# Attention with sigmoid weights: two of three score tiles read half by ScalarE and half by VectorE, last rows of scores written ahead of the last rows of values

## The chip, the cores and the metric

One core of a Trainium2 chip. The time is the device time of one execution in microseconds (us), as the median of several runs; the kernel before takes 871.62 us (median of 3 runs, 871.44 to 872.32). One further execution was profiled.

## What is computed

A batch of 8 with 12 heads of 448 positions and head size 64 goes through an attention whose weights are sigmoids, and the result through a layer that takes the largest of three products:

```python
scores = scale * np.matmul(q, k.transpose(0, 1, 3, 2)) - np.log(S)
attn = 1.0 / (1.0 + np.exp(-scores))
attn_out = np.matmul(attn, v)
x = attn_out.transpose(0, 2, 1, 3).reshape(B * S, H * D)
h = np.maximum(np.maximum(x @ w1, x @ w2), x @ w3)
out = h @ w_out
```

A sigmoid has no row maximum and no row sum, so each score can be turned into a weight by itself as soon as it is there.

## The kernel before

The kernel has two phases. The first is the attention, the second (lines 448 to 599) the layer of products, split into blocks that are combined with seven products each. All calls go through `pin`, which keeps the instructions of each engine in the order in which the program writes them; the framework adds the semaphores. An instruction of an engine therefore waits for everything that stands ahead of it on that engine, whatever it needs itself.

The attention runs over 24 "fours" (line 363): a batch element and four heads, that is two pairs of heads g = 0 and 1. The 448 positions of keys are three chunks of 128 and a rest of 64. For each pair and chunk, `scores` (L324) writes a tile `ps_s` of 128 keys by 2 heads by 448 queries into PSUM; each head has a bank of its own (the tile is `[P, 2, 512]` in 4-byte values). It takes three terms of two matmuls, since q and k are split into a high and a low part (`qk_split`, L316, a CAST and a TENSOR_TENSOR on VectorE). The rest of all four heads goes into one tile, `last_scores` (L335). There are three buffers of `ps_s`, taken in turn:

```python
ps_s = pool(stack, "ps_s", 3, space=PSUM)
```

A score tile becomes weights by a sigmoid on ScalarE, straight out of PSUM (`sigmoid`, L309, at L311), or is first copied to SBUF by VectorE (`raw_scores`, L379, at L382) and turned into weights there, in place, later (`raw_sigmoid`, L386). A buffer is free for the score tile three further on once its reader has finished. The weights are multiplied with the values by `weigh` (L347, chunks, at L349) and `last_weigh` (L354, rest, at L358) into two tiles `ps_av`, which `finish` (L369) copies to SBUF on VectorE (L374) and stores to DRAM on the queue of SP (L375).

The loop is staggered. Iteration n starts with the scores of the second pair of n (tiles s0, s1, s2), then come those of the first pair of n + 1 (f0, f1, f2), then all `weigh` of n, then `last_weigh` of n, then the last scores of n + 1 (L), then `finish` of n. So seven score tiles go round three buffers in each iteration: s2 takes the buffer of L, f0 that of s0, f1 that of s1, f2 that of s2. ScalarE reads L, s0, s2, f0, f1 and f2; VectorE reads s1.

Between these, VectorE also splits weights of the second phase (L156, L157, in some iterations) and decodes the weights that come as 64-bit words (L180 to L189), with two steps of the decode on ScalarE (L178, L179). The loads of values (L306), of queries and keys (L301) and of raw weights (L168) stand in the same queue of SP as the stores of `finish`. In the last iteration ScalarE and VectorE make the high and low parts of the first operands of the second phase (L263, L267), behind the sigmoids and the decode of that iteration.

Of the kernel before, what the change touches and what calls it, by code (L numbers as in the profile page):

```python
# [12 lines left out]
AF = mybir.ActivationFunctionType  # L13
# [26 lines left out]
def attention_then_maxout(  # L40
# [31 lines left out]
    nc = tc.nc  # L72
    B, NK = qk.shape[0], qk.shape[1]
    S = qk.shape[3] // 2
# [4 lines left out]
    scale = 1.0 / math.sqrt(D)  # L79
    neg_log_s = -math.log(S)  # L80
    pin = tc.keep_in_program_order

    const = ctx.enter_context(tc.tile_pool(name="const", bufs=1))
    bias_s = const.tile([P, 1], F32, name="bias_s")
# [10 lines left out]
    def pool(stack, name, bufs, **kw):  # L95
        return stack.enter_context(tc.tile_pool(name=name, bufs=bufs, **kw))
# [4 lines left out]
    m_p = pool(ctx, "m", 1)  # L101
# [169 lines left out]
    def attention(stack):  # L271
# [32 lines left out]
        def load_v(b, f):  # L304
            t = v_p.tile([P, 14, D], F32, name="v")
            pin(nc.sync.dma_start(out=t, in_=v[b, f]))  # L306
            return t

        def sigmoid(ps):  # L309
            a = a_p.tile([P, 2, S], F32, name="a")  # L310
            pin(nc.scalar.activation(  # L311
                out=a, in_=ps[:, :, :S], func=AF.Sigmoid, bias=bias_s, scale=scale
            ))
            return a
# [9 lines left out]
        def scores(terms, c):  # L324
            ps = ps_s.tile([P, 2, 512], F32, name="ps_s")
            for n, (kt, qt) in enumerate(terms):
                for e in range(2):
                    r = slice(e * D, (e + 1) * D)
                    pin(nc.tensor.matmul(
                        ps[:, e, :S], kt[r, S + c * P : S + (c + 1) * P], qt[r, :S],  # L330
                        start=n == 0, stop=n == len(terms) - 1,
                    ))
            return ps

        def last_scores(ts):  # L335

            ps = ps_s.tile([P, 2, 512], F32, name="ps_s")
            for g, t in enumerate(ts):
                for e in range(2):
                    r = slice(e * D, (e + 1) * D)  # L340
                    pin(nc.tensor.matmul(  # L341
                        ps[g * D : (g + 1) * D, e, :S], t[r, S + C * P :], t[r, :S],
                        start=True, stop=True,
                    ))
            return ps

        def weigh(ps, vt, g, c, a):  # L347
            for e in range(2):
                pin(nc.tensor.matmul(  # L349
                    ps[e * D : (e + 1) * D, :S], vt[:, (g * C + c) * 2 + e], a[:, e],  # L350
                    start=c == 0, stop=False,
                ))

        def last_weigh(pss, vt, a):  # L354
            for g, ps in enumerate(pss):
                r = slice(g * D, (g + 1) * D)
                for e in range(2):
                    pin(nc.tensor.matmul(  # L358
                        ps[e * D : (e + 1) * D, :S], vt[r, 4 * C + e], a[r, e],
                        start=False, stop=True,  # L360
                    ))

        fours = [(b, f) for b in range(B) for f in range(NK // 2)]

        def load(n):
            b, f = fours[n]
            return load_qk(b, 2 * f), load_qk(b, 2 * f + 1)

        def finish(n, pss, pool=m_p, names=("m11", "m12")):  # L369
            b, f = fours[n]  # L370
            for g, ps in enumerate(pss):
                k = 2 * f + g
                o = pool.tile([P, S], F32, name=names[g])
                pin(nc.vector.tensor_copy(out=o, in_=ps[:, :S]))  # L374
                pin(nc.sync.dma_start(  # L375
                    out=x_dram[k // HALF][:, k % HALF, b * S : (b + 1) * S], in_=o
                ))

        def raw_scores(ps):  # L379

            a = a_p.tile([P, 2, S], F32, name="a")
            pin(nc.vector.tensor_copy(out=a, in_=ps[:, :, :S]))  # L382
            return a

        def raw_sigmoid(a):
            pin(nc.scalar.activation(out=a, in_=a, func=AF.Sigmoid, bias=bias_s, scale=scale))  # L386

        def split_weights():
            for _ in range(2):
                if splits:  # L390
                    w_split(*splits.pop(0), nc.vector.tensor_copy)

        xs, count = {}, len(fours)
        ts, vt = load(0), load_v(*fours[0])
        next_ts = load(1)
        first = [sigmoid(scores([(ts[0],) * 2], c)) for c in range(C)]
        second_terms = qk_split(ts[1])
        decode()
        last = sigmoid(last_scores(ts))
        for n in range(count):  # L400
            ahead = n + 1 < count
            if ahead:
                next_vt = load_v(*fours[n + 1])
                later_ts = load(n + 2) if n + 2 < count else None
            if n == 0:
                first_terms = qk_split(next_ts[0])
            second = [None] * C
            second[0] = sigmoid(scores(second_terms, 0))
            second[1] = raw_scores(scores(second_terms, 1))
            second[2] = sigmoid(scores(second_terms, 2))  # L410
            if ahead:
                second_terms = qk_split(next_ts[1])
                next_first = [sigmoid(scores(first_terms, 0))]
            raw_sigmoid(second[1])
            split_weights()
            decode()
            if ahead:
                next_first += [sigmoid(scores(first_terms, c)) for c in range(1, C)]
            if n + 2 < count:
                first_terms = qk_split(later_ts[0])  # L420

            part = n - 9
            if 0 <= part < 4 * HALF:
                k, block = divmod(part, 4)
                row, th = ((0, 1), (0, 0), (1, 1), (1, 0))[block]
                x_block(xs, x_dram, 0, row, th, k)
                x_combine(xs, ((), ("t1",), ("t2", "t3"), ("t4",))[block], (k,))
            if n == count - 1:
                t_store(xs, 0)
                for name in FIRST:  # L430
                    x_lo(*x_hi(name, xs))
            pss = [ps_av.tile([P, 512], F32, name=f"ps_av{g}") for g in range(2)]
            for g, weights in enumerate((first, second)):
                for c in range(C):
                    weigh(pss[g], vt, g, c, weights[c])
            last_weigh(pss, vt, last)
            if ahead:
                last = sigmoid(last_scores(next_ts))
                finish(n, pss)
                vt, first, next_ts = next_vt, next_first, later_ts  # L440
        assert not splits
        return xs, lambda *to: finish(len(fours) - 1, pss, *to)

    with ExitStack() as stack:
        xs, finish = attention(stack)
# [68 lines left out]
    for n, (st, p) in enumerate(visits):  # L514
        nst, np_ = visits[n + 1] if (n, 2, 0) in his else (None, None)
        if nst in (1, 2):
            xs = x_load_all(np_)
        m = {}
        for q in range(3):
            ps, p1, u2, u3 = {}, None, None, None  # L520
# [37 lines left out]
            for k, (wname, xname, bank) in enumerate(PRODUCTS):  # L558
                here = n, q, k
                first = k < 4 or bank == 1  # L560
# [34 lines left out]
                if here == (n, 0, 4) and nst in (0, LAST):  # L595
                    xs = x_load(x_dram if nst == 0 else h_dram, np_)
# [45 lines left out]
```

## Time and profile before

| | |
|---|---|
| median of 3 runs | 871.62 us |
| profiled execution | 871.12 us, of which the span of instructions 869.3 |
| busy over the span | PE 860.6 (99%), PEld 693.9 (80%), DVE 647.2 (74%), ACT 393.4 (45%), POOL 182.3 (21%) |
| attention phase | up to about 258 us |
| granted clock of TensorE | full in all 40 slices |

PE is TensorE's matmuls, PEld its loads of weights, DVE is VectorE, ACT ScalarE, POOL GpSimd, SP the queue that issues the transfers. Times of rows in order of time are a start and a duration, in us from the start of the span. In a row of groups the last parts are: number of instructions | busy us, mean ns of one | idle time of the engine before them, with what ended it. In brackets behind a row of the timeline stands the idle time before it and what ended it. Matmuls overlap, and their ends are modelled, so that the start of a matmul and the waits of the loads of weights say more than busy time.

### The profile page before, as it was taken

The page shows a single profiled execution, that of the slowest core. Times are in us where ns is not written, and L with a number is a line of the kernel's source. Part 1 is how long each engine was busy: PE and PEld are TensorE (multiplying, and loading weights), DVE is VectorE, ACT ScalarE, POOL GpSimd, SP SyncE. Part 2 cuts the span into 40 slices and gives each one's busy share as a digit, 9 for nine tenths or more (in the row PEclk, how much of TensorE's full clock was granted, in tenths as well). Part 3 has the DMA queues.
Part 4 walks back from the last instruction along what each step waited for, and adds up shares of the span by engine and source line. Part 5 has one row for each costly group of instructions (what it writes and reads, how often), then busy time and mean ns, then how long its engine had stood idle before and what let it go on. Part 6 is the DMA issues. An engine that isn't in the chain of part 4 may idle for free. (4 is left out here: it accounts for less than half of the span.)

```text
span 869.3 us, 12929 instructions
## 1 busy us (share of the span) xinstructions
PE 860.6 (99%) x4842; PEld 693.9 (80%) x4842; DVE 647.2 (74%) x899; ACT 393.4 (45%) x499; POOL 182.3 (21%) x148
## 2 busy tenths in 40 slices
PE   8999999999999999999999999999999999999998
PEld 4555454555449999999999999999999998999997
DVE  5788778877876858689696879869687797737452
ACT  6777777776672414342253444225334352423320
POOL 0100022012102662602100020210002363760700
PEclk9999999999999999999999999999999999999999
DMA  6666667776637464414846542484563516262422
GB/s 248 211 230 233 226 238 251 250 250 236 227 127 276 177 246 156 178 52 132 305 145 234 217 170 79 138 302 151 222 231 135 169 58 210 103 213 98 164 77 85
DMA packets 74478, 161.87 MB, mean 186 GB/s; under 512 B 6960, under 2 KB 53936, under 8 KB 74416
## 3 DMA queue, kind: packets, MB, share of 16 engines
q1 hardware_dynamic: 74272, 160.94, 52.1%
q8 instruction: 38, 0.62, 0.3%
q14 instruction: 24, 0.20, 0.1%
q10 hardware_dynamic: 144, 0.11, 0.0%
HBM read 109.90 MB, written 51.12 MB: 185 GB/s over the span
## 5 line engine op out<-in xcount | busy, mean ns | idle before, releaser
L311 ACT ACTIVATE a<-ps_s,bias_s 128x896 f32<-128x896 f32 x144 | 137.4, 1006 | 75.4 <-PE ps_s L341 67.9
L458 PE MATMUL ps_y<-xlo_t,whi_s 128*128 128x448 f32 x432 | 156.8, 363 | 0.0
L458 PE MATMUL ps_y<-xhi_t,wlo_s 128*128 128x448 f32 x432 | 156.6, 363 | 0.0
L458 PE MATMUL ps_y<-xhi_t,whi_s 128*128 128x448 f32 x432 | 155.9, 361 | 0.0
L349 PE MATMUL ps_av<-a,v 128*64 128x448 f32 x576 | 113.5, 543 | 0.0
L458 PE MATMUL ps_y<-xlo_b,whi_a 128*128 128x448 f32 x288 | 104.6, 363 | 0.0
L458 PE MATMUL ps_y<-xhi_b,wlo_a 128*128 128x448 f32 x288 | 104.5, 363 | 0.0
L458 PE MATMUL ps_y<-xhi_b,whi_a 128*128 128x448 f32 x288 | 103.9, 361 | 0.0
L144 POOL TENSOR_TENSOR ws_s<-ws_a,ws_a 128x384 f32<-128x384 f32 x12 | 12.9, 1072 | 404.3 <-DMA ws_a<-w_dram 309.4
L568 ACT COPY p<-ps_y 128x448 f32<-128x448 f32 x48 | 25.5, 531 | 157.4 <-PE ps_y L458 144.8
L349 PEld LDWEIGHTS ps_av<-a,v 128*64 128x64 f32 x576 | 39.2, 137 | 63.0 <-issue 59.4
L458 PEld LDWEIGHTS ps_y<-xhi_t,wlo_s 128*128 128x128 f32 x432 | 81.1, 188 | 5.8
L458 PEld LDWEIGHTS ps_y<-xhi_t,whi_s 128*128 128x128 f32 x432 | 80.9, 187 | 5.6
L458 PEld LDWEIGHTS ps_y<-xlo_t,whi_s 128*128 128x128 f32 x432 | 81.1, 188 | 4.6
L542 DVE TENSOR_TENSOR m<-ps_y,u 128x448 f32<-128x448 f32 x71 | 43.8, 621 | 51.6 <-PE ps_y L458 47.3
L232 POOL TENSOR_TENSOR xs_t<-xs_b,xs_t 128x448 f32<-128x448 f32 x48 | 64.6, 1370 | 39.1 <-DMA xs_b<-x_dram 38.7
L571 DVE TENSOR_TENSOR u<-ps_y,p 128x448 f32<-128x448 f32 x48 | 29.9, 623 | 51.8 <-PE ps_y L458 47.9
L267 DVE TENSOR_TENSOR xlo_b<-xs_b,xhi_b 128x1344 fp32r<-128x1344 f32 x42 | 68.2, 1623 | 0.0
L267 DVE TENSOR_TENSOR xlo_t<-xs_t,xhi_t 128x1344 fp32r<-128x1344 f32 x42 | 67.6, 1610 | 0.0
L540 ACT COPY m<-ps_y 128x448 f32<-128x448 f32 x24 | 12.8, 533 | 119.1 <-PE ps_y L458 111.1
L178 ACT ACTIVATE c<-wraw 128x384 f32<-128x384 f32 x48 | 26.7, 556 | 76.4 <-DVE m L548 45.5
L263 ACT CAST xhi_t<-xs_t 128x1344 fp32r<-128x1344 f32 x42 | 55.3, 1316 | 11.9 <-PE ps_y L458 7.1
(68 smaller groups left out, 1677.2 us busy)
## 6 DMA issues: line engine op xcount, KB each, us to landing
qk<-qk SPq DMA_DIRECT2D x48, 448.0 KB, 5.3
xs_b<-x_dram SPq DMA_DIRECT2D x30, 672.0 KB, 6.5
wraw<-w SPq DMA_DIRECT2D x36, 384.0 KB, 6.6
xs_t<-t_dram SPq DMA_DIRECT2D x18, 672.0 KB, 7.8
v<-v SPq DMA_DIRECT2D x24, 448.0 KB, 3.7
h_dram<-m SPq DMA_DIRECT2D x48, 224.0 KB, 1.9
xs_b<-h_dram SPq DMA_DIRECT2D x16, 672.0 KB, 6.3
outT<-m SPq DMA_DIRECT2D x47, 224.0 KB, 2.0
```

The lines of the kernel that those rows point to most:

```text
L144: pin(nc.gpsimd.tensor_tensor(out=r[name], in0=r[in0], in1=r[in1], op=op))
L178: pin(nc.scalar.activation(out=square, in_=high.bitcast(F32), func=AF.Square))
L232: pin(nc.gpsimd.tensor_tensor(out=r[name][:, k], in0=r[in0][:, k], in1=r[in1][:, k], op=ALU.subtract))
L263: pin(nc.scalar.copy(out=hi, in_=r[name]))
L267: pin(nc.vector.tensor_tensor(out=lo, in0=x, in1=hi.bitcast(F32), op=ALU.subtract))
L311: pin(nc.scalar.activation(out=a, in_=ps[:, :, :S], func=AF.Sigmoid, bias=bias_s, scale=scale))
L349: pin(nc.tensor.matmul(ps[e * D : (e + 1) * D, :S], vt[:, (g * C + c) * 2 + e], a[:, e], start=c == 0, stop=False,))
L458: pin(nc.tensor.matmul(ps[:, :S], wt[:, k * P : (k + 1) * P], xt[:, k], start=first and n == 0, stop=n == len(terms) - 1, skip_group_check ...
L540: pin(nc.scalar.copy(out=m[name], in_=y))
L542: pin(nc.vector.tensor_tensor(out=m[name], in0=y, in1=add, op=ALU.add))
L568: pin(nc.scalar.copy(out=p1, in_=ps[0][:, :S]))
L571: pin(nc.vector.tensor_tensor(out=u2, in0=ps[1][:, :S], in1=p1, op=ALU.add))
```

## The change

Four things change, all in the attention loop.

- s0 and s2 are read by two engines: VectorE copies the second head's half to SBUF, and ScalarE turns the first head's half into weights (`shared_scores`). The half that was copied gets its sigmoid in place later; that makes two such sigmoids of half the size in place of one.
- s1 is read by ScalarE alone, as the other tiles are.
- `last_scores` of n + 1 stands ahead of `last_weigh` of n, where it stood behind it.
- `finish` of n stands no longer at the end of iteration n but in iteration n + 1, one half behind the copy of s0 and the other behind the copy of s2. Its stores move with it in SP's queue, behind the loads of values, queries and keys of that iteration.

```diff
--- before.py
+++ after.py
@@ -366,31 +366,38 @@
             b, f = fours[n]
             return load_qk(b, 2 * f), load_qk(b, 2 * f + 1)
 
-        def finish(n, pss, pool=m_p, names=("m11", "m12")):
+        def finish(n, pss, pool=m_p, names=("m11", "m12"), gs=range(2)):
+            if n < 0:
+                return
             b, f = fours[n]
-            for g, ps in enumerate(pss):
+            for g in gs:
                 k = 2 * f + g
                 o = pool.tile([P, S], F32, name=names[g])
-                pin(nc.vector.tensor_copy(out=o, in_=ps[:, :S]))
+                pin(nc.vector.tensor_copy(out=o, in_=pss[g][:, :S]))
                 pin(nc.sync.dma_start(
                     out=x_dram[k // HALF][:, k % HALF, b * S : (b + 1) * S], in_=o
                 ))
 
-        def raw_scores(ps):
+        def shared_scores(ps):
 
             a = a_p.tile([P, 2, S], F32, name="a")
-            pin(nc.vector.tensor_copy(out=a, in_=ps[:, :, :S]))
+            pin(nc.vector.tensor_copy(out=a[:, 1], in_=ps[:, 1, :S]))
+            pin(nc.scalar.activation(
+                out=a[:, 0], in_=ps[:, 0, :S], func=AF.Sigmoid, bias=bias_s, scale=scale
+            ))
             return a
 
         def raw_sigmoid(a):
-            pin(nc.scalar.activation(out=a, in_=a, func=AF.Sigmoid, bias=bias_s, scale=scale))
+            pin(nc.scalar.activation(
+                out=a[:, 1], in_=a[:, 1], func=AF.Sigmoid, bias=bias_s, scale=scale
+            ))
 
         def split_weights():
             for _ in range(2):
                 if splits:
                     w_split(*splits.pop(0), nc.vector.tensor_copy)
 
-        xs, count = {}, len(fours)
+        xs, count, pss = {}, len(fours), None
         ts, vt = load(0), load_v(*fours[0])
         next_ts = load(1)
         first = [sigmoid(scores([(ts[0],) * 2], c)) for c in range(C)]
@@ -405,13 +412,16 @@
             if n == 0:
                 first_terms = qk_split(next_ts[0])
             second = [None] * C
-            second[0] = sigmoid(scores(second_terms, 0))
-            second[1] = raw_scores(scores(second_terms, 1))
-            second[2] = sigmoid(scores(second_terms, 2))
+            second[0] = shared_scores(scores(second_terms, 0))
+            finish(n - 1, pss, gs=(0,))
+            second[1] = sigmoid(scores(second_terms, 1))
+            second[2] = shared_scores(scores(second_terms, 2))
+            finish(n - 1, pss, gs=(1,))
             if ahead:
                 second_terms = qk_split(next_ts[1])
                 next_first = [sigmoid(scores(first_terms, 0))]
-            raw_sigmoid(second[1])
+            raw_sigmoid(second[0])
+            raw_sigmoid(second[2])
             split_weights()
             decode()
             if ahead:
@@ -433,11 +443,10 @@
             for g, weights in enumerate((first, second)):
                 for c in range(C):
                     weigh(pss[g], vt, g, c, weights[c])
+            next_last = sigmoid(last_scores(next_ts)) if ahead else None
             last_weigh(pss, vt, last)
             if ahead:
-                last = sigmoid(last_scores(next_ts))
-                finish(n, pss)
-                vt, first, next_ts = next_vt, next_first, later_ts
+                vt, first, next_ts, last = next_vt, next_first, later_ts, next_last
         assert not splits
         return xs, lambda *to: finish(len(fours) - 1, pss, *to)
```

What this makes of the order of instructions, at three places of the middle of the loop. Behind a row stands in brackets for which engines' semaphores the instruction waits (PE_49 for TensorE, DVE_49 for VectorE, Activation_49 for ScalarE, DMAHW for a transfer); a wait that another wait already implies is not written.

ScalarE from L on, before: `a_1545` is L, then come s0, s2 and f0, the sigmoid in place of s1 and the two steps of the decode.

```order
L311 ACTIVATE a_1545<-ps_s_1540,bias_s_58 128x896 [waits PE_49,Activation_49]
L311 ACTIVATE a_1566<-ps_s_1559,bias_s_58 128x896 [waits PE_49,Activation_49]
L311 ACTIVATE a_1584<-ps_s_1577,bias_s_58 128x896 [waits PE_49,Activation_49]
L311 ACTIVATE a_1597<-ps_s_1590,bias_s_58 128x896 [waits PE_49]
L386 ACTIVATE a_1575<-a_1575,bias_s_58 128x896 [waits DVE_49,Activation_49]
L178 ACTIVATE c_1610<-wraw_1366 128x384 [waits DMAHW3_49]
L179 ACTIVATE wraw_1366<-wraw_1366 128x384
```

After: L, the half of s0, s1, the half of s2, f0, the two sigmoids in place, the decode.

```order
L311 ACTIVATE a_1577<-ps_s_1572,bias_s_58 128x896 [waits PE_49,Activation_49]
L385 ACTIVATE a_1596<-ps_s_1589,bias_s_58 128x448 [waits DVE_49,Activation_49]
L311 ACTIVATE a_1609<-ps_s_1602,bias_s_58 128x896 [waits PE_49]
L385 ACTIVATE a_1618<-ps_s_1611,bias_s_58 128x448 [waits DVE_49,Activation_49]
L311 ACTIVATE a_1635<-ps_s_1628,bias_s_58 128x896 [waits PE_49]
L391 ACTIVATE a_1596<-a_1596,bias_s_58 128x448
L391 ACTIVATE a_1618<-a_1618,bias_s_58 128x448
L178 ACTIVATE c_1649<-wraw_1399 128x384 [waits DMAHW3_49]
L179 ACTIVATE wraw_1399<-wraw_1399 128x384
```

The full reads of s0 and s2 became halves, and the read of s1 came in between them. The two halves wait for VectorE, not for TensorE.

VectorE from the split of the first pair on, before: CAST and TENSOR_TENSOR of the split, the two copies of `finish`, the copy of s1, the next split.

```order
L320 CAST hi_1397<-qk_1321 128x896 [waits DMAHW1_49,PE_49]
L321 TENSOR_TENSOR lo_1398<-qk_1321,hi_1397 128x896 [waits DVE_49]
L374 COPY m11_1430<-ps_av0_1405 128x448 [waits DMAHW6_49,PE_49]
L374 COPY m12_1433<-ps_av1_1406 128x448 [waits DMAHW7_49,PE_49]
L382 COPY a_1458<-ps_s_1451 128x896 [waits PE_49]
L320 CAST hi_1469<-qk_1323 128x896 [waits DMAHW2_49,PE_49]
L321 TENSOR_TENSOR lo_1470<-qk_1323,hi_1469 128x896 [waits DVE_49]
```

After:

```order
L320 CAST hi_1549<-qk_1465 128x896 [waits DMAHW6_49,PE_49]
L321 TENSOR_TENSOR lo_1550<-qk_1465,hi_1549 128x896 [waits DVE_49]
L384 COPY a_1596<-ps_s_1589 128x448 [waits PE_49]
L376 COPY m11_1599<-ps_av0_1558 128x448 [waits DMAHW0_49]
L384 COPY a_1618<-ps_s_1611 128x448 [waits PE_49]
L376 COPY m12_1621<-ps_av1_1559 128x448 [waits DMAHW1_49]
L320 CAST hi_1624<-qk_1467 128x896 [waits DMAHW7_49]
L321 TENSOR_TENSOR lo_1625<-qk_1467,hi_1624 128x896 [waits DVE_49]
```

The copies of `finish` moved behind those of s0 and s2, each of which has half the size of the one of s1.

TensorE at f0 and f1, before; the first row of each tile has the waits.

```order
L329 MATMUL ps_s<-hi 128x448 [waits DVE_49,Activation_49]
L329 MATMUL ps_s<-hi 128x448
L329 MATMUL ps_s<-lo,hi 128x448 [waits DVE_49]
L329 MATMUL ps_s<-lo,hi 128x448
L329 MATMUL ps_s<-hi,lo 128x448 x2
L329 MATMUL ps_s<-hi 128x448 [waits DVE_49]
L329 MATMUL ps_s<-hi 128x448
L329 MATMUL ps_s<-lo,hi 128x448 x2
L329 MATMUL ps_s<-hi,lo 128x448 x2
L329 MATMUL ps_s<-hi 128x448 [waits Activation_49]
```

After:

```order
L329 MATMUL ps_s<-hi 128x448 [waits Activation_49]
L329 MATMUL ps_s<-hi 128x448
L329 MATMUL ps_s<-lo,hi 128x448 x2
L329 MATMUL ps_s<-hi,lo 128x448 x2
L329 MATMUL ps_s<-hi 128x448 [waits Activation_49]
L329 MATMUL ps_s<-hi 128x448
L329 MATMUL ps_s<-lo,hi 128x448 x2
L329 MATMUL ps_s<-hi,lo 128x448 x2
L329 MATMUL ps_s<-hi 128x448 [waits Activation_49]
```

f1, whose buffer was s1's, waited for VectorE, and now waits for ScalarE; f0 waits for ScalarE in both.

## The prediction

> **What bounds the kernel now.** The change touches only the attention loop, so I read first what each engine waits for between 13 and 254 us, then one iteration of the loop in order of time, from one weigh to the next (160.74 to 171.27 us). I call the seven score tiles of an iteration s0, s1, s2 (second pair of heads), f0, f1, f2 (first pair of the next iteration) and L (last rows). Three rows of the waits (engine, line, what ended the wait: total, times, longest):
>
> ```profile
> ACT a L311 <- PE ps_s L341: 67.9, 23, 3.0
> DVE a L382 <- PE ps_s L329: 23.5, 23, 1.0
> PEld ps_s L329 <- ACT a L311: 12.7, 44, 0.5
> ```
>
> ScalarE and VectorE wait for TensorE in every iteration, so neither is full. TensorE's weight loads wait for ScalarE's reads of score tiles 44 times, about twice an iteration. These waits are all that the change could win. The stretch of one iteration confirms it:
>
> ```profile
> 160.74:171.27 10.53, 10.51 (x78) 5.30 (x77) 9.11 (x16) 7.44 (x10) 1.15 (x1) 1.00 0.72 250
> ```
>
> After the length the columns are busy PE, PEld, DVE, ACT and POOL. PE's 10.51 says little, as matmuls overlap; DVE has 1.42 us to spare, ACT 3.09. TensorE's own rows (start, duration) show its pace:
>
> ```profile
> 160.74 4.73 PE L349 MATMUL ps_av<-a,v 128*64 128x448 f32 x24
> 165.41 0.98 PE L358 MATMUL ps_av<-a,v 64*64 64x448 f32 x8
> 166.21 0.93 PE L341 MATMUL ps_s<-qk 64*64 64x448 f32 x8
> 167.07 0.47 PE L329 MATMUL ps_s<-hi 64*128 64x448 f32 x2
> ...
> 167.58 0.36 PE L329 MATMUL ps_s<-hi,lo 64*128 64x448 f32 x2
> 167.78 0.37 PE L329 MATMUL ps_s<-hi 64*128 64x448 f32 x2
> ...
> 168.19 0.37 PE L329 MATMUL ps_s<-hi,lo 64*128 64x448 f32 x2
> 168.40 0.43 PE L329 MATMUL ps_s<-hi 64*128 64x448 f32 x2
> ...
> 169.25 0.47 PE L329 MATMUL ps_s<-hi 64*128 64x448 f32 x2
> ...
> 169.96 0.37 PE L329 MATMUL ps_s<-hi 64*128 64x448 f32 x2
> ...
> 170.58 0.36 PE L329 MATMUL ps_s<-hi 64*128 64x448 f32 x2
> ...
> 171.27 0.60 PE L349 MATMUL ps_av<-a,v 128*64 128x448 f32 x2
> ```
>
> The rows with hi alone start s0 (167.07), s1 (167.78), s2 (168.40), f0 (169.25), f1 (169.96), f2 (170.58); those with hi,lo at 167.58 and 168.19 are the last pairs of s0 and s1. A tile that follows without a stall comes 0.61 to 0.62 after the one before (169.96 to 170.58). From s2 to f0 it is 0.85, and f0 itself, started afresh after a stall, takes 0.71 to f1. A loop without stalls is thus shorter by 0.24 + 0.10 = 0.34 us; more than that can't be won in an iteration of 10.53. The weight loads name the two stalls:
>
> ```profile
> 168.35 0.19 PEld L329 LDWEIGHTS ps_s<-hi 64*128 64x128 f32 x2 [0.17 <-ACT a L311]
> 169.25 0.19 PEld L329 LDWEIGHTS ps_s<-hi 64*128 64x128 f32 x2 [0.39 <-ACT a L311]
> ```
>
> Three score buffers go round: s2 takes L's, f0 takes s0's, f1 takes s1's, f2 takes s2's. The real stall is f0's, and it waits for the read of s0. The readers:
>
> ```profile
> 162.45 1.89 ACT L311 ACTIVATE a<-ps_s,bias_s 128x896 f32<-128x896 f32 x2
> 167.29 3.95 ACT L311 ACTIVATE a<-ps_s,bias_s 128x896 f32<-128x896 f32 x4 [2.95 <-PE ps_s L341]
> ...
> 165.28 1.09 DVE L321 TENSOR_TENSOR lo<-qk,hi 128x896 fp32r<-128x896 f32 x1
> 166.42 1.16 DVE L374 COPY m<-ps_av 128x448 f32<-128x448 f32 x2
> 168.60 1.09 DVE L382 COPY a<-ps_s 128x896 f32<-128x896 f32 x1 [1.02 <-PE ps_s L329]
> 169.61 0.62 DVE L320 CAST hi<-qk 128x896 fp32r<-128x896 f32 x1
> ```
>
> ScalarE reads L, s0, s2, f0 back to back from 167.29; VectorE meanwhile reads s1 alone. That is why f1 does not wait today: its buffer is free at 168.60 + 1.09 = 169.69, before 169.96.
>
> **The change part by part.** Durations, from the page and the groups by shape:
>
> ```profile
> L374 DVE COPY m<-ps_av 128x448 f32<-128x448 f32 x46 | 26.6, 620 | 9.9 <-PE ps_av L358 9.5
> L311 ACT ACTIVATE a<-ps_s,bias_s 128x896 f32<-128x896 f32 x144 | 137.4, 1006 | 75.4 <-PE ps_s L341 67.9
> L568 ACT COPY p<-ps_y 128x448 f32<-128x448 f32 x48 | 25.5, 531 | 157.4 <-PE ps_y L458 144.8
> ```
>
> VectorE's half copy has the shape of L374: 0.62. ScalarE's half sigmoid is not in the trace. From below: L568, same shape, a plain copy, 0.53. From above: the full sigmoid less 448 columns. A full copy of 1344 columns in the end rows below takes 1.30, so a column costs (1.30 − 0.53)/896 = 0.86 ns, 448 of them 0.39, and 1.01 − 0.39 = 0.62. I take 0.62, since it comes from the sigmoid's own row. Two ACTIVATEs in a row overlap by 2 x 1.01 − 1.89 = 0.12. From the end of a read to the stalled matmul pass 0.07 (L and s0: 167.29 + 2.01 − 0.12 = 169.18; f0 at 169.25). The Trainium skill ("ScalarE: Activation LUTs", What ACT_TABLE_LOAD costs) gives an ACTIVATE with a pointer bias 280 ns + 0.833 ns a column: 1.03 for 896, beside the row's 1.01, and 0.65 for the half; with it the sum below would come to 881.5.
>
> The halves are not read side by side. In the order of the changed program ScalarE's half waits for VectorE and for ScalarE and not for TensorE, whose scores it reads: it gets them through VectorE's copy of the other half, and starts when that copy has ended. What such a hand-over costs is shown by a c buffer in the second phase:
>
> ```profile
> 513.13 0.63 DVE L548 TENSOR_TENSOR m<-c,m 128x448 f32<-128x448 f32 x1
> ...
> 513.79 0.55 ACT L178 ACTIVATE c<-wraw 128x384 f32<-128x384 f32 x1 [5.08 <-DVE m L548]
> ```
>
> 0.03 us. Now the iteration again, on the same clock.
>
> Last rows ahead: L starts at 165.41 in place of 166.21, ScalarE reads it from 166.49 to 167.50, and the 0.17 before s2 goes. TensorE's forms follow one another as before, at no cost; the last values end where L ended, at 167.07.
>
> s0: its last pair at 167.58 gives VectorE a start 0.41 later, as s1's does (168.19 to 168.60): 167.99 to 168.61. ScalarE's half 168.64 to 169.26. f0 starts at 169.33; today 169.25. The stall stays, 0.08 longer.
>
> s1: ScalarE comes to it only behind the half of s0: 169.14 to 170.15. f1 starts at 170.22; today 169.96. This is a new wait: behind the waiting half in ScalarE's queue stands the whole read of s1.
>
> s2: its half runs 170.03 to 170.65, and f2 is reached at 170.22 + 0.71 = 170.93, restarted like f0; no wait. From f2 to the next weigh 0.69, as today: 171.62 against 171.27. Each iteration is **0.35 longer**. With 0.53 for the half it is 0.26, without the 0.10 of the restart 0.16; with no overlap behind the half 0.47.
>
> finish, moved behind the two half copies: 2 x 0.58 of VectorE from its idle stretch to behind s0 and between s0 and s2; s2's scores are ready at 168.40 + 0.41 + 0.41 = 169.22 and VectorE is through with the first finish at 168.53 + 0.62 = 169.15. Costs nothing; cover gone, s2's half on ScalarE has 0.2 to spare. In SP's queue the two stores to x_dram now stand behind the loads of v and qk, and the weight load behind the stores:
>
> ```profile
> 167.07 0.85 SPq L375 DMA_DIRECT2D x_dram<-m  x2
> ...
> 169.74 0.38 SPq L168 DMA_DIRECT2D wraw<-w  x1
> ```
>
> The weight load slips from 169.74 to behind the second store (VectorE ends it near 170.4), a microsecond or so; it is issued two iterations ahead. v and qk come earlier. Nothing. The sigmoid in place becomes two, some 0.25 more on ScalarE, inside its 3.09.
>
> The first iteration costs more. There the split of the next heads is still running on VectorE when s0 is ready:
>
> ```profile
> 9.37 1.09 DVE L321 TENSOR_TENSOR lo<-qk,hi 128x896 fp32r<-128x896 f32 x1
> 10.38 1.09 DVE L382 COPY a<-ps_s 128x896 f32<-128x896 f32 x1
> ...
> 12.98 0.97 PE L349 MATMUL ps_av<-a,v 128*64 128x448 f32 x4
> ```
>
> The half copy can start at 10.38: to 11.00, ScalarE's half to 11.65, s1 to 12.54, f1 at 12.61, weigh 0.71 + 0.69 later at 14.01, against 12.98: 1.03.
>
> The end: the second phase's second matmul waits for the low part of b11, that for its high part, that stands behind the sigmoids and the decode on ScalarE:
>
> ```profile
> 252.80 1.09 DVE L382 COPY a<-ps_s 128x896 f32<-128x896 f32 x1 [1.03 <-PE ps_s L329]
> ...
> 257.58 1.56 DVE L267 TENSOR_TENSOR xlo_b<-xs_b,xhi_b 128x1344 fp32r<-128x1344 f32 x1
> ...
> 254.42 1.03 ACT L386 ACTIVATE a<-a,bias_s 128x896 f32<-128x896 f32 x1
> 255.35 0.56 ACT L178 ACTIVATE c<-wraw 128x384 f32<-128x384 f32 x1
> ...
> 256.25 1.30 ACT L263 CAST xhi_b<-xs_b 128x1344 fp32r<-128x1344 f32 x1
> ...
> 259.22 0.45 PE L458 MATMUL ps_y<-xlo_b,whi_a 128*128 128x448 f32 x1
> ```
>
> 256.25 + 1.30 = 257.55, then 257.58 + 1.56 = 259.14, then 259.22: one chain. There s0's copy comes at 252.80 − 0.61 = 252.19; ScalarE's half runs 252.84 to 253.46, s1 to 254.35, s2's half to 254.85. The sigmoid in place (1.03, the next begins 0.10 before its end) becomes two of 0.64: they start at 254.73 and 255.27, the decode at 255.81 in place of 255.35. 0.46.
>
> Sum: 23 iterations have f tiles, the first counted by itself: 22 x 0.35 + 1.03 + 0.46 = 7.7 + 1.5 = 9.2. The profiled execution took 871.12 (span 869.3 and 1.8 around it), so 880.3; the median of the runs, 871.62, is 0.50 above it: **880.8**.
>
> **The rivals.** Faster: the halves do run side by side. Both start at 167.99, s0 is free at 168.61, f0 follows s2 without a stall at 169.01; s1 is read 168.60 to 169.61, f1 at 169.62 to 169.68. An iteration is 0.19 to 0.34 shorter, 23 of them 4.4 to 7.8: 863.8 to 867.2, 865.5 in the middle. It decides if ScalarE's half starts within 0.1 of VectorE's. The Trainium skill ("PSUM — Partial Sum Buffer", Specifications) says that ScalarE and VectorE can read it at once at full bandwidth without a bank collision; the halves lie in different banks, so by that rule alone this rival would win. Against it speak the waits in the order. 0.09.
>
> No change: the half costs only its columns, 0.39, and a stall only its lateness. Then f1 starts at 169.99, weigh follows 0.61 + 0.69 later at 171.29, and 22 x 0.02 + 0.8 leave 872.9 or less. Against it: L568's 0.53, and f0's 0.71 after each stall. 0.06.
>
> Slower still: VectorE becomes the bound. In iterations that split weights it is busy 9.11; one copy of 1.09 becomes two of 0.62, 9.26. Against 10.88 it has 1.6 to spare, and decides only past that; 0.3 more in some 11 iterations would give 884. 0.05.
>
> **How the numbers follow.** The forecast holds 0.80. Its range: low, 22 x 0.16 and the single terms at nothing, 871.62 + 3.5 = 875.1; high, 22 x 0.47 + 1.15 + 0.6 = 12.1, 883.7, and 884 with part of the last rival. Left out are the two rivals with 0.15 and some 0.03 at the rim. 0.2% is 1.7 us, about what a measurement of this kernel can tell from no change: faster 0.09, same 0.06, slower 0.85.
>
> **What would show it.** In the changed profile: ScalarE's half of s0 starts where VectorE's half ends, not beside it; weight loads wait for ScalarE at f0 by some 0.4 and anew at f1 by some 0.3, while the wait at s2 is gone; weigh to weigh is 10.88, the first weigh starts near 14.0. The prediction is wrong if the two halves start together, if f1 does not wait, or if the loop is not longer than 10.53.

## The result, and the profile after

The changed kernel takes **882.43 us** (median of 4 runs, 882.14 to 882.59) where the kernel before took 871.8 beside it (4 runs, 871.44 to 872.32). The ratio is 1.0121, with an interval of 1.0104 to 1.0139: slower, as forecast, and 1.6 us above the predicted 880.8.

The profiled execution took 882.43, with a span of 880.6 against 869.3 before: 11.3 us more. Where they went is read by cutting the span at four points: the start of the first split scores (s0 of the first iteration, on TensorE), the first weigh, the 23rd weigh (the last whose iteration has f tiles), and the end.

| stretch | before | after | difference | predicted |
|---|---|---|---|---|
| start to first s0 | 8.74 | 10.16 | +1.42 | 0 |
| first s0 to first weigh | 4.24 | 4.59 | +0.35 | 1.03 |
| 22 iterations, weigh to weigh | 231.96 | 241.05 | +9.09 | 7.7 |
| 23rd weigh to the end | 624.36 | 624.85 | +0.49 | 0.46 |

The four differences add up to that, but for rounding. The row of the 22 iterations is 10.94 to 10.97 for each; before it was 10.51 to 10.53 in 20 of them, and 10.69 and 10.75 in two. One iteration by the view of windows (length, then busy time of PE, PEld, DVE, ACT and POOL, with the instructions in brackets):

```profile
157.20:168.15 10.95, 10.69 (x78) 5.29 (x76) 9.16 (x17) 7.79 (x12) 0.00 (x0) 1.00 0.74 235
```

No engine has become full: VectorE 9.16 of 10.95, ScalarE 7.79, at a granted clock of 1.00. TensorE has the same 78 matmul rows and takes longer over them. The waits between 13 and 266 us (engine, line, what ended the wait: total, times, longest) say for what. L384 is VectorE's half copy, L385 ScalarE's half sigmoid, L311 the whole sigmoid:

```profile
ACT a L311 <- PE ps_s L341: 46.0, 23, 2.0
DVE a L384 <- PE ps_s L329: 41.6, 23, 3.1
ACT a L385 <- DVE a L384: 27.2, 23, 1.2
...
PEld ps_s L329 <- ACT a L385: 13.4, 22, 0.6
...
PEld ps_s L329 <- ACT a L311: 9.1, 23, 0.4
```

ScalarE's half of s0 waits 23 times for VectorE's half, 1.2 us each, and never for TensorE, whose scores it reads. In the loop TensorE's weight loads then wait for that half (0.6) and for a whole read (0.4): two stalls an iteration. The same in order of time (start, duration; in brackets the idle time before and what ended it), from s0 at 163.52 to the weigh at 168.15:

```profile
163.52 0.47 PE L329 MATMUL ps_s<-hi 64*128 64x448 f32 x2
...
164.44 0.62 DVE L384 COPY a<-ps_s 128x448 f32<-128x448 f32 x1 [1.38 <-PE ps_s L329]
...
165.16 0.63 ACT L385 ACTIVATE a<-ps_s,bias_s 128x448 f32<-128x448 f32 x1 [1.18 <-DVE a L384]
...
165.69 1.00 ACT L311 ACTIVATE a<-ps_s,bias_s 128x896 f32<-128x896 f32 x1
165.84 0.19 PEld L329 LDWEIGHTS ps_s<-hi 64*128 64x128 f32 x2 [0.61 <-ACT a L385]
...
166.58 0.64 ACT L385 ACTIVATE a<-ps_s,bias_s 128x448 f32<-128x448 f32 x1
...
166.74 0.19 PEld L329 LDWEIGHTS ps_s<-hi 64*128 64x128 f32 x2 [0.40 <-ACT a L311]
...
168.15 0.20 PEld L349 LDWEIGHTS ps_av<-a,v 128*64 128x64 f32 x4 [0.30 <-issue]
```

VectorE's half of s0 ends at 164.44 + 0.62 = 165.06, ScalarE's starts at 165.16 and ends at 165.79; f0 comes at 165.84. The read of s1, ready long before, starts at 165.69 behind that half, and f1 waits for it until 166.74.

### The profile page after: what moved, and what is told of

Read it like the earlier page. It is cut to its first block, busy times and chain, and to the rows that moved or that the text cites. A ratio compares the mean times of both kernels' runs of the same rounds, so it can differ in the third digit from the quotient of the medians.

```text
span 880.6 us, 12858 instructions
## 1 busy us (share of the span) xinstructions
PE 866.2 (98%) x4842; PEld 694.1 (79%) x4842; DVE 648.8 (74%) x923; ACT 401.4 (46%) x547; POOL 182.5 (21%) x148
## 5 line engine op out<-in xcount | busy, mean ns | idle before, releaser
L311 ACT ACTIVATE a<-ps_s,bias_s 128x896 f32<-128x896 f32 x120 | 118.7, 1013 | 51.1 <-PE ps_s L341 46.4
L144 POOL TENSOR_TENSOR ws_s<-ws_a,ws_a 128x384 f32<-128x384 f32 x12 | 14.7, 1221 | 410.3 <-DMA ws_a<-w_dram 309.8
L329 PE MATMUL ps_s<-hi 64*128 64x448 f32 x282 | 58.9, 415 | 5.7 <-ACT a L385 5.1
L384 DVE COPY a<-ps_s 128x448 f32<-128x448 f32 x48 | 30.0, 625 | 44.2 <-PE ps_s L329 42.8
```

The lines of the kernel that those rows point to most:

```text
L144: pin(nc.gpsimd.tensor_tensor(out=r[name], in0=r[in0], in1=r[in1], op=op))
L311: pin(nc.scalar.activation(out=a, in_=ps[:, :, :S], func=AF.Sigmoid, bias=bias_s, scale=scale))
L329: pin(nc.tensor.matmul(ps[:, e, :S], kt[r, S + c * P : S + (c + 1) * P], qt[r, :S], start=n == 0, stop=n == len(terms) - 1,))
L384: pin(nc.vector.tensor_copy(out=a[:, 1], in_=ps[:, 1, :S]))
```

## The experiments

All times beside the kernel before on the same chip; the ratios have a 95% interval. The loop is the distance from weigh to weigh.

| kernel | what it has of the change | median us | ratio | loop us |
|---|---|---|---|---|
| before_again | nothing (one run) | 872.0 | – | 10.53 |
| swap_only | last scores ahead of last values | 870.26 | 0.9972 [0.9961, 0.9983] | 10.41 |
| finish_only | finish and its stores moved | 872.74 | 1.0000 [0.9991, 1.0009] | 10.54 |
| halves_only | halves, with s1 to ScalarE | 883.35 | 1.0123 [1.0110, 1.0137] | 10.97 |
| first_half | all, but s0 alone in halves | 876.33 | 1.0049 [1.0033, 1.0066] | 10.67 |
| scalar_first | all, ScalarE's half written first | 882.29 | 1.0109 [1.0094, 1.0124] | 10.90 |
| banks_apart | all, a PSUM tile for each half | 871.79 | 0.9990 [0.9981, 0.9999] | 10.48 |
| swap_banks | swap_only with a PSUM tile for each half | 872.64 | 1.0000 [0.9991, 1.0010] | 10.53 |
| three_halves | banks_apart, s1 in halves too, finish behind s2 | 865.81 | 0.9922 [0.9907, 0.9937] | 10.17 |
| after_again | all, as changed (one run) | 883.05 | – | 10.96 |

My theory is that of the prediction: the halves run one after the other, f0's stall stays, and s1's read, queued behind the waiting half, makes a second one. The rivals: that another of the four parts carries the loss, and that reading by two engines costs something in itself.

### One part at a time

**swap_only.** The last scores alone are moved:

```diff
+            next_last = sigmoid(last_scores(next_ts)) if ahead else None
             last_weigh(pss, vt, last)
             if ahead:
-                last = sigmoid(last_scores(next_ts))
+                last = next_last
```

> The kernel before with one part of the change: the last scores ahead of the last values. Theory (the loss is the waiting half): the read of L moves 0.80 us forward, so ScalarE comes to s0 when it is ready, 0.18 earlier than before; f0 starts 0.18 earlier, an iteration is 10.35 in place of 10.53, the time about 867.8. Rival (the new order on TensorE costs the time): an iteration of about 10.95 and some 881; if the order is worth nothing, 871.8.

It gave 870.26, 2.4 us less than the kernel before beside it (872.68), and a loop of 10.41 where I expected 10.35: the part does gain, two thirds of what I gave it. Four rows around s0 (at 166.35) and f0:

```profile
166.35 0.47 PE L329 MATMUL ps_s<-hi 64*128 64x448 f32 x2
...
167.32 1.01 ACT L311 ACTIVATE a<-ps_s,bias_s 128x896 f32<-128x896 f32 x1 [0.51 <-PE ps_s L329]
...
168.37 0.19 PEld L329 LDWEIGHTS ps_s<-hi 64*128 64x128 f32 x2 [0.32 <-ACT a L311]
168.38 0.47 PE L329 MATMUL ps_s<-hi 64*128 64x448 f32 x2
```

ScalarE is through with L before s0 is ready and reads s0 as soon as its scores are there; f0 comes 2.03 after s0, where it came 2.18 after it before. The stall shrinks but does not go.

**finish_only.** Only `finish` moves, with its stores:

```diff
             second[0] = sigmoid(scores(second_terms, 0))
+            finish(n - 1, pss, gs=(0,))
             second[1] = raw_scores(scores(second_terms, 1))
             second[2] = sigmoid(scores(second_terms, 2))
+            finish(n - 1, pss, gs=(1,))
...
-                finish(n, pss)
```

> The kernel before with one part of the change: the copies of finish stand one behind the read of s0 (nothing of VectorE's there) and so ahead of the copy of s1, the other behind s2, and their stores behind the loads. Theory: VectorE and SP have room, an iteration stays at 10.53, 871.1 to 872.5. Rival (the move of finish and of the stores makes part of the loss): an iteration of 10.6 to 10.9, 874 to 881.

872.74 against 872.68, loop 10.54: nothing, in VectorE's order as in SP's queue. (The 872.5 at the top of my range was set beside a kernel before of 871.8.)

**halves_only.** The halves and s1's whole read by ScalarE, with the last scores and `finish` where they were (the functions are those of the change):

```diff
-            second[0] = sigmoid(scores(second_terms, 0))
-            second[1] = raw_scores(scores(second_terms, 1))
-            second[2] = sigmoid(scores(second_terms, 2))
+            second[0] = shared_scores(scores(second_terms, 0))
+            second[1] = sigmoid(scores(second_terms, 1))
+            second[2] = shared_scores(scores(second_terms, 2))
```

> The kernel before with one part of the change: s0 and s2 read half by VectorE and half by ScalarE, s1 by ScalarE; finish and the last scores stay where they were. Theory: all of the loss in the loop is here, an iteration of 10.95, waits of the weight loads for ScalarE at f0 and f1, 881 to 882.5. Rival (the other two parts make the loss, or the three only together): 10.53 to 10.7, 872 to 876.

883.35, loop 10.97, both a little above what I expected. This part carries the whole loss, alone. It also shows that the swap, worth 0.12 an iteration by itself, is worth 0.01 beside the halves. The reason stands in this kernel's rows: s0 starts at 163.40, VectorE's half at 164.31 as soon as the scores are there, and ScalarE is through with L at 164.63, before VectorE's half hands over at 165.03. An earlier L frees ScalarE for nothing:

```profile
163.62 1.01 ACT L311 ACTIVATE a<-ps_s,bias_s 128x896 f32<-128x896 f32 x1 [2.80 <-PE ps_s L341]
...
164.31 0.62 DVE L384 COPY a<-ps_s 128x448 f32<-128x448 f32 x1 [0.41 <-PE ps_s L329]
...
165.03 0.63 ACT L385 ACTIVATE a<-ps_s,bias_s 128x448 f32<-128x448 f32 x1 [0.40 <-DVE a L384]
```

**first_half.** The changed kernel with s0 alone in halves; s1 goes back to VectorE, with a whole sigmoid in place later, and s2 whole to ScalarE:

```diff
             second[0] = shared_scores(scores(second_terms, 0))
-            finish(n - 1, pss, gs=(0,))
-            second[1] = sigmoid(scores(second_terms, 1))
-            second[2] = shared_scores(scores(second_terms, 2))
+            second[1] = raw_scores(scores(second_terms, 1))
+            finish(n - 1, pss, gs=(0,))
+            second[2] = sigmoid(scores(second_terms, 2))
             finish(n - 1, pss, gs=(1,))
```

> The changed kernel, but only s0 is read by two engines: s1 is copied whole by VectorE as in the kernel before, s2 read whole by ScalarE, and the two finish copies stand behind s1's and s2's. My theory: of the loss in an iteration, s0's late f0 is one part and s1's read, queued on ScalarE behind the waiting half, the other. Here f0 should still follow s0 by 2.33 us and wait for ScalarE, and f1 should not wait: 0.71 from f0 to f1, 0.61 to f2, 0.69 to the weigh, so 4.34 from s0 to the weigh in place of 4.63, weigh to weigh 10.66, and 22 x 0.30 less than the changed kernel: 875 to 877. Rival: f0's lateness, or the second reader as such, carries the whole loss; then the loop stays at 10.9 to 11.0 and the time at 881 to 884.

876.33 and a loop of 10.67, as the theory has it. From s0 (169.48) on:

```profile
169.48 0.47 PE L329 MATMUL ps_s<-hi 64*128 64x448 f32 x2
...
171.81 0.47 PE L329 MATMUL ps_s<-hi 64*128 64x448 f32 x2 [0.23 <-ACT a L385]
...
172.52 0.37 PE L329 MATMUL ps_s<-hi 64*128 64x448 f32 x2
...
173.13 0.36 PE L329 MATMUL ps_s<-hi 64*128 64x448 f32 x2
```

f0 follows s0 by 2.33 as in the changed kernel, f1 follows f0 by 0.71 and f2 follows f1 by 0.61, without a wait. Counted from swap_only, which has the new order and no halves, the loss of an iteration thus has two parts of about the same size: s0's halves in turn (10.41 to 10.67, 0.26) and the second stall, from handing s1 to ScalarE (10.67 to 10.96, 0.28: f1 later by 0.18, and f2 by a further 0.10, since f1 starts afresh after its stall).

### The halves in turn, or side by side

**scalar_first.** In `shared_scores` ScalarE's half is written ahead of VectorE's:

```diff
+            pin(nc.scalar.activation(
+                out=a[:, 0], in_=ps[:, 0, :S], func=AF.Sigmoid, bias=bias_s, scale=scale
+            ))
             pin(nc.vector.tensor_copy(out=a[:, 1], in_=ps[:, 1, :S]))
-            pin(nc.scalar.activation(
-                out=a[:, 0], in_=ps[:, 0, :S], func=AF.Sigmoid, bias=bias_s, scale=scale
-            ))
```

> The changed kernel with ScalarE's half written ahead of VectorE's, in one tile as in the change: now VectorE waits for ScalarE. Theory (two halves of one tile are read one after the other, and what stands behind the waiting half in its queue is late): f0 stalls as in the change, since the sum of the halves is the same; ScalarE comes to s1 0.6 earlier, so f1 doesn't stall, but VectorE's copy of s2 now ends late and f2 stalls by 0.2; an iteration of 10.80 to 10.90, 879 to 882, waits of TensorE for VectorE in place of those for ScalarE. Rival (only the size of the halves and the number of instructions matter, or the two halves can be read together in one order): 10.95 and unchanged at 882.4, or below 10.6.

882.29, loop 10.90, just past the upper rim of the time I expected. Now VectorE waits for ScalarE, and TensorE for VectorE (L384 is here ScalarE's half, L387 VectorE's):

```profile
163.62 0.64 ACT L384 ACTIVATE a<-ps_s,bias_s 128x448 f32<-128x448 f32 x1 [0.52 <-PE ps_s L329]
...
164.17 1.01 ACT L311 ACTIVATE a<-ps_s,bias_s 128x896 f32<-128x896 f32 x1
...
164.28 0.62 DVE L387 COPY a<-ps_s 128x448 f32<-128x448 f32 x1 [1.06 <-ACT a L384]
...
164.96 0.19 PEld L329 LDWEIGHTS ps_s<-hi 64*128 64x128 f32 x2 [0.60 <-DVE a L387]
...
166.41 0.19 PEld L329 LDWEIGHTS ps_s<-hi 64*128 64x128 f32 x2 [0.33 <-DVE a L387]
```

So neither engine as such is slow to start: whichever half the program has second waits for the first. And the s1 part of the loss goes away here, as ScalarE reads s1 at 164.17 and f1 does not wait. A new wait takes its place at f2, for VectorE's half of s2, which comes behind ScalarE's half, and that behind ScalarE's read of s1.

**banks_apart.** What ties the halves? They share the tile that they read, `ps_s`, and the one that they write, `a`. Here each head's scores get a PSUM tile of their own, one bank each; `a` stays one tile, and all else is as in the changed kernel:

```diff
-            ps = ps_s.tile([P, 2, 512], F32, name="ps_s")
+            ps = [ps_s.tile([P, 512], F32, name=f"ps_s{e}") for e in range(2)]
...
-            pin(nc.vector.tensor_copy(out=a[:, 1], in_=ps[:, 1, :S]))
+            pin(nc.vector.tensor_copy(out=a[:, 1], in_=ps[1][:, :S]))
             pin(nc.scalar.activation(
-                out=a[:, 0], in_=ps[:, 0, :S], func=AF.Sigmoid, bias=bias_s, scale=scale
+                out=a[:, 0], in_=ps[0][:, :S], func=AF.Sigmoid, bias=bias_s, scale=scale
             ))
```

A whole tile is read by two ACTIVATEs of half the size.

> The changed kernel with each score tile made of two tiles of one bank, so that no wait ties the half of ScalarE to that of VectorE; full reads become two ACTIVATEs, one for each bank, some 0.14 more for each tile on ScalarE. Theory: with the wait gone the halves start together, f0 and f1 don't stall or by under 0.1, an iteration of 10.17 to 10.35, 864 to 869. Rival (not the wait, but the number of instructions and their fixed costs lose the time, or the two engines slow each other in PSUM): an iteration of 10.9 or more, 882 and above.

871.79, loop 10.48: from a ratio of 1.0121 down to 0.9990 by this alone. The rows after s0 (166.95), with L385 VectorE's half and L386 ScalarE's:

```profile
167.89 0.62 DVE L385 COPY a<-ps_s 128x448 f32<-128x448 f32 x1 [0.89 <-PE ps_s L330]
167.91 0.64 ACT L386 ACTIVATE a<-ps_s,bias_s 128x448 f32<-128x448 f32 x1 [0.35 <-PE ps_s L330]
...
168.88 0.36 PE L330 MATMUL ps_s<-hi 64*128 64x448 f32 x2
...
169.49 0.67 PE L330 MATMUL ps_s<-hi 64*128 64x448 f32 x2
...
169.68 0.18 PEld L330 LDWEIGHTS ps_s<-hi 64*128 64x128 f32 x1 [0.21 <-ACT a L312]
```

Both halves start within 0.02 us of each other, both wait for TensorE, and take 0.62 and 0.64, as they did one at a time: two engines reading two banks cost each other no more than 0.01 here. f0 starts without a stall at 168.88. But the loop is not the 10.17 to 10.35 that I expected, nor the time the 864 to 869. s1 is still read by ScalarE alone, and the second head's half of it comes free a little late: at f1 one of the pair's two weight loads waits 0.21. From there the two heads' matmuls are out of step (f1 to f2 takes 0.72, f2 to the weigh 0.88; in a loop without waits 0.61 and 0.69).

**swap_banks.** To see what a tile for each half does without the halves, the same is done to swap_only; VectorE then copies s1 in two pieces:

```diff
-            pin(nc.vector.tensor_copy(out=a, in_=ps[:, :, :S]))
+            for e in range(2):
+                pin(nc.vector.tensor_copy(out=a[:, e], in_=ps[e][:, :S]))
```

> swap_only with each score tile made of two tiles of one bank, all read by the same engines as before, in two instructions. Theory (as f1 in banks_apart: the second head's matmul waits alone, and the two heads' matmuls then no longer run side by side): f0's second head waits some 0.2 for the second half of s0, and the tiles behind it take 0.73 and 0.88; an iteration of 10.40 to 10.50, no gain over swap_only, 869.5 to 872. Rival (a bank that is free earlier is a gain): 10.2 to 10.3, 865 to 867.

872.64, loop 10.53, both just above what I expected. Separate tiles by themselves gain nothing, and even lose what the swap had gained: here too a single weight load of a pair waits (0.27 at 170.43) and the heads fall out of step. The gain of banks_apart over the changed kernel comes from the halves, no longer tied.

**three_halves.** What is left in banks_apart is s1's read on one engine. Here s1 is shared as s0 and s2 are:

```diff
             second[0] = shared_scores(scores(second_terms, 0))
-            finish(n - 1, pss, gs=(0,))
-            second[1] = sigmoid(scores(second_terms, 1))
+            second[1] = shared_scores(scores(second_terms, 1))
             second[2] = shared_scores(scores(second_terms, 2))
-            finish(n - 1, pss, gs=(1,))
+            finish(n - 1, pss)
```

A third half sigmoid in place follows from it, and both copies of `finish` now stand behind the copy of s2; that a move of `finish` gains nothing by itself is what finish_only showed.

> As banks_apart, but s1 too is read half by VectorE and half by ScalarE, and both copies of finish stand behind s2's. Theory (a stall of f1 comes from ScalarE's whole read of s1, which no engine shares): s1 is free 0.65 after it is ready, no score tile waits, an iteration of 10.17 to 10.25 in place of 10.48, 863.5 to 866.5. Rival (VectorE is full with three half copies, or ScalarE with the many small ones): 10.4 or more, 869 and above.

865.81, **0.9922 [0.9907, 0.9937]**: faster than both kernels, 7 us under the one before. VectorE and ScalarE read three halves each, side by side, and s2, f0 and f1 follow without a stall; the row of the window holds one iteration:

```profile
164.20 1.84 DVE L385 COPY a<-ps_s 128x448 f32<-128x448 f32 x3
164.23 1.85 ACT L386 ACTIVATE a<-ps_s,bias_s 128x448 f32<-128x448 f32 x3 [0.35 <-PE ps_s L330]
...
165.19 0.36 PE L330 MATMUL ps_s<-hi 64*128 64x448 f32 x2
...
165.80 0.36 PE L330 MATMUL ps_s<-hi 64*128 64x448 f32 x2
```

```profile
156.93:167.10 10.17, 10.17 (x77) 5.45 (x77) 9.80 (x19) 8.61 (x17) 0.18 (x1) 1.00 0.79 271
```

The loop of 10.17 is 0.36 shorter than the 10.53 before, about what the prediction named as all that can be won (0.34). VectorE is busy 9.80 of it and would be next in line. The last iteration gives a little back: its weigh waits 1.3 us that the others don't, because it waits for VectorE: the first copy of `finish`, which frees its `ps_av`, stands behind the three half copies and ends at 247.98, and the weigh starts at 248.05.

### The start

**before_again** and **after_again** are the two kernels unaltered, for the 1.42 us at the start.

> The kernel before, unchanged, profiled once more, for the start. Theory (how long TensorE's first matmuls run slowly differs from one execution to the next, whatever the kernel): the first split scores start at another time than 8.74, between 8.7 and 10.2, with an iteration of 10.53 again. Rival (the start belongs to the program): 8.74 within 0.1.

> The changed kernel once more, unaltered. Theory: the late start of the first split scores in its profile (10.16 us against 8.74) belongs to the execution and not to the change: another profile should have them anywhere between 8.7 and 10.4, with the same loop of 10.96. Rival: it belongs to the change, and they start at 10.1 to 10.2 again.

The loops came out as they had (10.53 and 10.96). The first s0 started at 9.17 in the one and at 10.35 in the other. Over all twelve profiles it lies between 8.74 and 10.39, when all of them have run the same operations (the kernels with a tile for each half read them in two pieces): the first twelve matmuls of raw scores take 3.98 to 4.85 us from the first start to the last end. The first row of TensorE before, and of the changed kernel:

```profile
3.82 4.08 PE L329 MATMUL ps_s<-qk 64*128 64x448 f32 x12 [3.82 <-DMA qk<-qk]
```

```profile
3.99 4.85 PE L329 MATMUL ps_s<-qk 64*128 64x448 f32 x12 [3.99 <-DMA qk<-qk]
```

first_half has the changed program up to s1 and took 4.20 and 9.23; three_halves took 4.85 and 10.39. So the halves do not set it. But both profiles of the changed kernel are late (10.16, 10.35) and both of the kernel before early (8.74, 9.17); two of each don't settle whether that is chance or belongs to the program, and it stays open. If it is chance, up to 1.4 of the 10.6 us between the medians is no loss of the change; the 9.09 of the loop is. For after_again the 10.35 lies in the theory's range, at its rim, and just above the rival's 10.1 to 10.2; it decides nothing.

## Why the prediction was right, step by step

- **The halves are not read side by side**: right, and shown three ways. ScalarE's half waits for VectorE's (1.18 before 165.16); with the order turned round VectorE waits for ScalarE (1.06); with a PSUM tile for each half both start together. The halves lie in different banks in all of these, so it is the shared tile that ties them, not the banks.
- **The price of a half**, 0.62 estimated for ScalarE from the whole sigmoid less its columns: 0.63 and 0.64 in the rows. By the Trainium skill ("ScalarE: Activation LUTs", What ACT_TABLE_LOAD costs), 280 ns and 0.833 ns a column, it would be 0.65, a little above these rows.
- **The hand-over was too cheap.** The step "0.03 us", taken from a c buffer in the second phase, is the term that was mis-sized in the loop: from the end of VectorE's half to the start of ScalarE's it is 165.16 − 165.06 = 0.10. f0 therefore comes 2.33 after s0 and not the 2.26 worked out. The 0.03 holds for another kind of wait. In the first iteration of the changed kernel the hand-over takes 0.04 (11.08 + 0.62 = 11.70, then 11.74 in the rows further down), in each of the 23 others 0.09 to 0.10; after_again, halves_only and first_half show the same two values. The first half of all waits for VectorE alone. The later ones wait for VectorE and for ScalarE's own semaphore, as the order of the changed program shows, and the trace has one more semaphore instruction on line 385 for each of them (46 for 48 halves). At the c buffer the other wait, for a load, had ended 4.7 us before. So the second wait goes with some 0.06 more; no run changed it by itself. The rest of the iteration came as written: f1 0.89 later (predicted 0.89), f2 0.71 (0.71), weigh 0.70 (0.69). The loop is 10.96 and not 10.88; in 22 iterations that is 1.7 us, of which 0.3 are had back, as the two long iterations of before are gone.
- **f1's new wait**: right, 0.40 by the weight loads where some 0.3 was named. first_half shows its cause: with s1 back on VectorE it is gone.
- **"The 0.17 before s2 goes"**: the wait went, but no time hung on it. Between the starts of s1 and s2 stand 0.62 before, 0.60 after; the wait now stands ahead of f0 (0.17 + 0.39 before, 0.61 after). What the swap does gain alone, 0.12, it gains by ScalarE's earlier start on s0, and beside the halves that has no use.
- **finish and SP's queue at nothing**: right, finish_only is at 1.0000.
- **The first iteration**, 1.03 predicted, 0.35 measured. The step that failed is that "the split of the next heads is still running on VectorE when s0 is ready". s0 itself came 1.42 later, the split did not, and so it was over in time:

```profile
9.47 1.09 DVE L321 TENSOR_TENSOR lo<-qk,hi 128x896 fp32r<-128x896 f32 x1
...
11.08 0.62 DVE L384 COPY a<-ps_s 128x448 f32<-128x448 f32 x1 [0.52 <-PE ps_s L329]
...
11.74 0.63 ACT L385 ACTIVATE a<-ps_s,bias_s 128x448 f32<-128x448 f32 x1 [0.39 <-DVE a L384]
...
14.75 0.60 PE L349 MATMUL ps_av<-a,v 128*64 128x448 f32 x2
```

  VectorE idled 0.52 before its half copy, and the first weigh came at 14.75. From s0 on, the first iteration lost 0.35, a little less than each other one (0.41 on average). In first_half, where s0 started at 9.23, the step does hold: VectorE's half copy starts at 10.32, straight behind the split (9.31 + 1.09) and 0.17 after s0's scores. So it hangs on how early s0 starts, which one profile could not tell.
- **The end**: 0.46 predicted, 0.49 measured, by the chain that was named: the second matmul of the second phase comes 0.80 after the first, where it came 0.31 after it.
- **The faster rival** needed ScalarE's half within 0.1 of VectorE's. It starts 0.72 after it (165.16 against 164.44). By the rule cited there, in "PSUM — Partial Sum Buffer", Specifications, of the Trainium skill, the two engines can read at once; banks_apart agrees with it to 0.02 us. The rule was right about the memory, and the changed program doesn't get to use it. The rival of no change needed a half at the price of its columns, 0.39; it took 0.63. The rival with VectorE as the bound did not come up: 9.16 of 10.95.

Against the profile the sum was 2.1 us low: the loop by 1.4, nearly all of it the hand-over, and the start by 1.42, less 0.7 of the first iteration. The median is 1.6 above the prediction, since 0.5 had been added for the distance of median and profile, and the changed kernel has none. The start was in no term of the sum, and could not have been worked out from one profile. That the total came so close is in part luck: the 0.7 and the 0.5 make up for some of what the loop and the start added. The way and the mechanism do not hang on it.

## What to carry to other kernels

Splitting a tile between two engines pays only if they can start together: look at what the second reader waits for before counting its half as parallel, and give each engine a tile of its own where the framework ties readers of one tile. Separate tiles gain nothing by themselves (swap_banks, 1.0000). A read that waits in an engine's queue delays everything queued behind it, so price the tile behind it as well as the one that is split. A gain seen alone (the swap, 0.12 an iteration) can be worth nothing beside another change that moves the wait elsewhere.

## What the runs showed of the hardware

- A hand-over from VectorE to ScalarE through a tile took 0.10 us (164.44 + 0.62 to 165.16) where the reader waited for a second semaphore too, and 0.04 (11.08 + 0.62 to 11.74) where it did not; one from ScalarE to VectorE, with one wait, took 0.02 by the rows of scalar_first (163.62 + 0.64 to 164.28), 0.03 by its trace in ns.
- Score matmuls go in pairs, one head in each half of TensorE's rows. When one weight load of a pair waits and the other does not, 0.21 us in banks_apart, later tiles don't make up for it: f1 to f2 takes 0.72 and f2 to the weigh 0.88, where 0.61 and 0.69 are to be had. In swap_banks a wait of 0.27 at f0 costs 0.37 up to the weigh (2.28 from 170.18 to 172.46, where 1.91 is to be had).
- The first matmuls run at about half pace (in the kernel before one pair follows another by 0.75 us from 4.73 to 6.97, and by 0.39 after that; a pair's weight loads take 0.34 us at 4.73 and 0.20 at 6.97). For how long differs between executions: 3.98 to 4.85 us for the same twelve, with a granted clock of 1.00 over the first 20 us of both kernels. The Trainium skill ("TensorE: Matmul & The Clock Gate", Part 1: The HAM clock gate) says that the array starts cold and warms up after a free-running window of about 3.4 us, so that the switch depends on where in the window the first matmul falls. That the length differs agrees with this. The length itself goes past one window: some 3.1 us in the kernel before (3.82 to 6.97), over 4.7 in the changed one, where the last scores at 8.77 still take 1.46 us (0.98 before) and the first matmul was at 3.99. No run here varied where in the window it falls.
